# Attention beside an MLP on one core: the last six steps, the order of the last four units, and the projection as a chain

## The chip, the cores and the metric

The kernel runs on one core of one Trainium2 chip. The metric is the device time in microseconds of one execution; the median of the runs shown below is the time before. The profile is one profiled execution; its rows give microseconds from the start of the span, which runs from the first to the last instruction.

## The reference, cut to what matters

Both branches start from `x` (2048 tokens, 576 features) and are mixed by a gate per token:

```python
g = _sigmoid((x * gate_w).sum(-1, keepdims=True))
qkv = (x @ wqkv).reshape(B, S, 3, 32, 18)              # q, k, v of 32 heads of 18
p = _softmax(einsum("bhqd,bhkd->bhqk", q, k) * 18**-0.5)
a = einsum("bhqk,bhkd->bhqd", p, v) (heads joined) @ wo
y = _layernorm(x)
b = _gelu(y @ w1 + b1) @ w2 + b2                       # 576 -> 4608 -> 576
return g * a + (1 - g) * b
```

All is float32. The kernel splits operands into a rounded part and a rest and adds three products of them for one float32 product, so that a matmul line of the code stands for three passes.

## The kernel before, in words

**Prologue.** The first part computes q, k and v for all tokens and stores them to scratch in DRAM (`qk_scr`, `v_scr`), normalizes `x` and stores that too (`y_scr`). It ends where the attention loop begins.

**The loop.** Heads are taken in 16 pairs. A unit `u` is one pair and one half of the queries (1024 of them), so there are 32 units: `unit(u)` gives pair `u // 2` and half `u % 2`. Each unit has 16 steps `kc`, one for each 128 keys; `step` counts through all 512. A step makes scores with `s2` (L236, tile `pss`) and the exponential on ScalarE (L238, into `p` or `ring`). Every second step also runs `pv` (L253, 16 matmuls), which multiplies the probabilities of two steps with v. What follows calls the stretch from one `pv` to the next a double step: 256 of them make the loop. The row maxima that the exponential needs come one unit ahead, from `next_round` (matmul L195, maximum on VectorE L197); when a unit's are complete they are turned by one matmul (L212) and written into the query tile by four small DMAs (`qa<-mr`), which the first scores of the next unit wait for. The score tile `pss` exists once, so scores, exponential and next scores alternate.

**Tiles of the loop.** Queries lie in three tiles `QA`, keys in two tiles `KA` (pair modulo 2), values in two tiles `VT`. `o_store` copies a finished unit's sums out (`oe`), sends them to `ot_scr`, gathers the sums of the exponentials (`dn<-oe`), takes reciprocals on VectorE (L276), writes them out (`dn_scr<-dn`) and spreads them over the rows of all 18 features (`wide`, `ot_scr<-dn_scr`). The two steps behind it wait 24 and 16 slots of `run_due`, in the last two units 4 and 4.

**The MLP beside it.** `mlp()` is a generator; `fill` takes one piece of it three times in each double step. For each of 4 blocks of 512 tokens and 9 groups of the hidden width there are two `h_pair` (L441, 54 matmuls each, weights `w`, tokens `big`) and four `out_pair` (L521, 24 times two matmuls each). A double step holds a whole `h_pair` (54 matmuls, three pieces), or half of one (28, then 26, five pieces over two double steps), or one `out_pair` (48 matmuls). The rule for the first cut is time: `behind` is the MLP time that should have been spent by this step if it were to end at step `FIN`, and an `h_pair` that isn't late is cut into five:

```python
behind[0] = base + (TOTAL - base) * step / FIN        # in fill; FIN = 500
late = spent[0] < behind[0]
if last and piece[0] == 0 and not late:
    ends = {4, 9, 14, 18, 23}
```

Between two blocks the next block's tokens are read in 12 DMAs (`big<-y_scr`).

**The projection.** `out_proj` multiplies the attention output with `wo`. For each block `b` of 512 tokens it loads the sums (`load_o`) and the reciprocals (`load_den`), multiplies and splits them in five chunks (`normed`: VectorE L941, ScalarE L945, VectorE L952), and then runs 8 groups of 14 matmuls (L999), each evicted by VectorE with gate and MLP output (L1003). That makes 32 groups, 448 matmuls. Before, it is appended to the stream when the MLP is done, its loads are tied to four fixed steps, and it takes 3 groups (`PEND`) up to the end of the loop. Block 0 waits until the first 31 units are stored, blocks 2 and 3 until all are. The chunks 0 to 3 are the rows 0 to 511 of `ot_scr`; chunk 4 is the rows 512 to 575, which with the pair size of 36 rows belong to pairs 14 and 15.

**Order of the work.** Nothing is scheduled by a planner: the instructions of each engine run in the order in which the code issues them. `run_due` is called after each piece of the loop (a slot), and it runs what `defer` and `bg` have queued. All DMAs but the output's go through SyncE's queue in that order, so one that waits holds those behind it.

Of the kernel before, what the change touches and what calls it, by code (L numbers as in the profile page):

```python
# [22 lines left out]
NT = S // P  # L23
NB = 4
# [14 lines left out]
PEND = 3  # L39
WAIT = 0.25  # L40
NSL = 1
# [4 lines left out]
PLAN = [[(), (0,), (1,), (2,), (3,), (4,), (5, 6), ()], [(), (), (0,), (1,), (2,), (3,), (4,), (5, 6)],  # L46
        [(0,), (1,), (2,), (3,), (4,), (5,), (6,), ()]]
NORM = 8
# [5 lines left out]
NSTEP = 512  # L54
FIN = NSTEP - 12


@with_exitstack
def gated_mix_kernel(ctx: ExitStack, tc: tile.TileContext, x, wqkv, wo, w1, b1, w2, b2, gate_w, out):
# [36 lines left out]
    KA = [att.tile([P, S], F32R, name=f"ka{i}") for i in range(2)]  # L96
# [33 lines left out]

    def run_due(ns=SLOT):

        slot[0] += 1
        now[0] += ns
        due = [f for t, f in timed if t <= now[0]]
# [21 lines left out]
    NU = 2 * NPAIR  # L157
    NR = 32

    def unit(u):  # L160
        return u // 2, u % 2
# [10 lines left out]
    def load_k(pair, c0=0, c1=S):  # L172
        ka = KA[pair % 2]
# [11 lines left out]
    def s1_round(u, r):  # L185
# [5 lines left out]
        qa, ka = QA[u % 3], KA[u // 2 % 2]  # L191
# [36 lines left out]
    def s2(u, kc, qb):  # L228
        qa, ka = QA[u % 3], KA[u // 2 % 2]
# [12 lines left out]
    def pv(n):  # L242
# [4 lines left out]
        v = VT[u // 2 % 2]  # L247
# [12 lines left out]
    def o_store(u, ps):  # L260
# [14 lines left out]
        def spread():  # L275
            nc.vector.reciprocal(dn, dn)  # L276
            nc.sync.dma_start(dn_scr[u], dn)
            defer(16 if u < NU - 2 else 4, wide)
# [5 lines left out]
        defer(24 if u < NU - 2 else 4, spread)  # L284
# [15 lines left out]
    def mlp():  # L300
# [35 lines left out]
        def more_raws():  # L336

            more = cw.tile([P, 2, D], F32, name="wlast")
            for c in (2, 3):
                R2.append(more[:, c - 2, :])  # L340
# [76 lines left out]
        def h_pair(q, last, inner=False):  # L417
# [17 lines left out]
            if last and piece[0] == 0 and not late:  # L435
# [161 lines left out]
    opening = []  # L597
    stream = [mlp()]
# [33 lines left out]
    with ExitStack() as a:  # L632
# [160 lines left out]
        for i in range(2):  # L793

            nc.gpsimd.memset(VT[i], 0.0)
            for j in range(2):
                nc.gpsimd.memset(VT[i][:, :, 19 * j + 18:19 * j + 19], 1.0)
                nc.gpsimd.memset(KA[i][64 * j + 32:64 * j + 64, :].bitcast(F32), 1.0)
# [75 lines left out]
    hooks = []  # L874
# [3 lines left out]
    def out_proj():  # L878

        wbig = big_tile().rearrange("p a b -> p (a b)").rearrange("p (c n) -> p c n", n=D)  # L880
        wlast = cw.tile([P, 2, D], F32R, name="wlast")
        raw = x_tile().rearrange("p (c n) -> p c n", n=640)[:, :, :D]

        def w_part(hl, c):
            return wbig[:, 5 * hl + c, :] if 5 * hl + c < 8 else wlast[:, c - 3, :]

        def split(c):
            src = raw[:, c % 4, :]
            nc.gpsimd.tensor_scalar(w_part(0, c), src, 1.0, 1.0, op0=ALU.mult, op1=ALU.mult)
            nc.gpsimd.tensor_tensor(w_part(1, c), src, w_part(0, c).bitcast(F32), op=ALU.subtract)  # L890

        def load_last():
            for h in range(2):
                nc.sync.dma_start(raw[64 * h:64 * h + 64, 0, :], wo[512:576, :])

        nc.sync.dma_start(raw, wo[0:512, :].rearrange("(c p) n -> p c n", p=P))
        bg.append((lambda: 0, lambda: split(0), SLOT))
        bg.append((lambda: 0, load_last, SLOT))
        for c in range(1, 5):
            bg.append((lambda: 0, lambda c=c: split(c), SLOT))  # L900
        OT, BT, done = {}, {}, {}

        def load_o(b):

            o = x_tile().rearrange("p (c n) -> p c n", c=5)
            cols = slice(b * TB, (b + 1) * TB)
            nc.sync.dma_start(o[:, 0:4, :], ot_scr[0, 0:512, cols].rearrange("(c p) n -> p c n", p=P))
            for h in range(2):
                nc.sync.dma_start(o[64 * h:64 * h + 64, 4, :], ot_scr[0, 512:576, cols])
            OT[b] = [o]  # L910
            done[b] = 0

        def load_den(b):

# [184 lines left out]
```

## Time and profile before

| | us |
|---|---|
| median of 3 runs (lowest, highest) | 2386.05 (2380.69, 2387.30) |
| the profiled execution | 2386.83 |
| its span | 2385.1 |
| TensorE busy | 2317.6 (97%) |
| VectorE, ScalarE, GpSimd busy | 1648.9, 1365.1, 964.5 |
| the chain that ended last: share of TensorE | 89% |

The profiled execution is 0.78 us above the median, and 1.73 us of it lie outside its span. In a row of the timeline stand the start, the length, the engine, the line of the code, the operation with output and inputs, the number of instructions merged into the row, and in brackets the idle time before it with what ended it. Rows that give a stretch of time list the stretch, its length, the busy time of TensorE's matmuls, of its weight loads, of VectorE, ScalarE and GpSimd with the number of instructions, the granted TensorE clock (1.00 is full speed), the share of the DMA engines and GB/s.

### The profile page before, as it was taken

What the parts mean: (1) busy time and instruction counts of PE and PEld (TensorE: products, weight loads), DVE (VectorE), ACT (ScalarE), POOL (GpSimd) and SP (SyncE); (2) the same over time, 40 slices, a digit from 0 to 9 for tenths busy, and PEclk for the clock granted to TensorE, in tenths of its full rate; (3) what the DMA queues carried; (4) which work ended last, traced back from release to release, by engine and by line L of the source; (5) the groups of instructions that cost most, each with busy time, mean ns of one, the idle gap of its engine ahead of it and who ended that gap; (6) DMA issues with size and microseconds to landing.
All of it is one profiled execution on the core that took longest, in us unless ns stands there. A gap on an engine that the chain in (4) does not pass through costs nothing.

```text
span 2385.1 us, 50611 instructions
## 1 busy us (share of the span) xinstructions
PE 2317.6 (97%) x20585; PEld 1618.2 (68%) x20585; DVE 1648.9 (69%) x2890; ACT 1365.1 (57%) x1604; POOL 964.5 (40%) x964
## 2 busy tenths in 40 slices
PE   8998899999999999999999999999999999999978
PEld 6876566666666666666666666666666676666638
DVE  5675577777777777777777777777766777777424
ACT  4222476666666665666666666666655666666551
POOL 3000466665555333344444443333433344444400
PEclk9999899999999999999999999999999999999989
DMA  7747936544355425242354423232645342331146
GB/s 232 244 145 202 266 130 183 165 144 140 127 157 161 145 93 155 95 132 94 114 153 142 127 97 112 87 112 93 160 117 185 100 124 96 101 126 68 61 149 205
DMA packets 164638, 330.40 MB, mean 139 GB/s; under 512 B 57742, under 2 KB 84402, under 8 KB 153570
## 3 DMA queue, kind: packets, MB, share of 16 engines
q1 hardware_dynamic: 161414, 321.71, 43.5%
q10 hardware_dynamic: 2992, 5.46, 0.6%
q8 instruction: 162, 2.65, 0.5%
q14 instruction: 70, 0.57, 0.1%
HBM read 234.31 MB, written 96.73 MB: 139 GB/s over the span
## 4 chain that ended last, share of the span: by engine, by line
PE 89%; DVE 3%; DMA 3%; ACT 2%; issue 1%; POOL 1%; SPq 0%; ACTq 0%; DVEq 0%; POOLq 0%
PE ps L521 20%; PE ps L253 19%; PE ps L441 17%; PE pss L236 12%; PE ps L195 11%; PE ps L758 4%; PE ps L776 2%; PE ps L999 2%; DVE m L197 1%; ACT p L238 1%; PE ps L682 1%; DMA vt<-v_scr 1%; DMA qa<-mr 0%; DMA big<-y_scr 0%; DVE p L742 0%
## 5 line engine op out<-in xcount | busy, mean ns | idle before, releaser
L197 DVE TENSOR_REDUCE m<-ps 128x1 f32<-128x512 f32 x2048 | 1298.7, 684 | 448.4 <-PE ps L195 447.3
L238 ACT ACTIVATE p<-pss 128x1024 f32<-128x1024 f32 x684 | 701.0, 1025 | 471.3 <-PE pss L236 457.8
L441 PE MATMUL ps<-big,w 64*128 64x512 f32 x3888 | 518.7, 393 | 3.2 <-DMA big<-y_scr 3.1
L154 POOL TENSOR_SCALAR zz<-zz 128x512 f32<-128x512 f32 x288 | 178.3, 619 | 829.7 <-ACT zz L494 727.3
L521 PE MATMUL ps<-w,hh 64*128 64x288 f32 x4352 | 497.1, 299 | 12.0 <-ACT z L462 0.3
L236 PE MATMUL pss<-qa,ka 56*128 56x512 f32 x2048 | 481.5, 437 | 25.3 <-ACT p L238 13.8
L238 ACT ACTIVATE ring<-pss 128x1024 f32<-128x1024 f32 x340 | 348.5, 1025 | 241.2 <-PE pss L236 236.0
L195 PE MATMUL ps<-ka,qa 54*128 54x512 f32 x2048 | 457.9, 410 | 6.2 <-DVE m L197 2.6
L521 PEld LDWEIGHTS ps<-w,hh 64*128 64x128 f32 x4352 | 398.5, 185 | 68.0 <-issue 44.6
L441 PEld LDWEIGHTS ps<-big,w 64*128 64x128 f32 x3888 | 394.0, 185 | 68.1 <-DMA big<-y_scr 3.9
L236 PEld LDWEIGHTS pss<-qa,ka 56*128 56x128 f32 x2048 | 198.0, 185 | 281.4 <-ACT p L238 127.3
L154 POOL TENSOR_TENSOR zz<-zz,z 128x512 f32<-128x512 f32 x288 | 371.6, 1290 | 24.1
L253 PE MATMUL ps<-p,vt 128*32 128x512 f32 x2736 | 351.2, 608 | 0.4 <-DMA vt<-v_scr 0.4
L521 PE MATMUL ps<-w,hl 64*128 64x288 f32 x2176 | 349.0, 292 | 0.0
L195 PEld LDWEIGHTS ps<-ka,qa 54*128 54x128 f32 x2048 | 239.7, 185 | 36.1 <-DVE m L197 11.9
L521 PEld LDWEIGHTS ps<-w,hl 64*128 64x128 f32 x2176 | 233.8, 185 | 0.3
L154 POOL TENSOR_TENSOR w<-x,w 128x1152 fp32r<-128x1152 f32 (+1 forms) x36 | 73.1, 2044 | 325.9 <-ACT w L357 312.6
L253 PE MATMUL ps<-ring,vt 128*32 128x512 f32 x1360 | 181.4, 606 | 0.0
L154 POOL TENSOR_TENSOR hl<-zz,hh 128x512 fp32r<-128x512 f32 x136 | 176.6, 1299 | 11.4
L253 PEld LDWEIGHTS ps<-p,vt 128*32 128x32 f32 x2736 | 72.1, 110 | 151.7 <-issue 150.3
L530 DVE SCALAR_TENSOR_TENSOR x<-ps,x 128x288 f32<-128x288 f32 x256 | 105.1, 452 | 33.2 <-PE ps L521 19.6
L758 PE MATMUL ps<-big,wqk 128*128 128x512 f32 x504 | 126.8, 405 | 0.8 <-DVE wqk L676 0.5
(95 smaller groups left out, 1363.3 us busy)
## 6 DMA issues: line engine op xcount, KB each, us to landing
w<-w_scr SPq DMA_DIRECT2D x54, 1152.0 KB
w<-w_scr SPq DMA_DIRECT2D x108, 576.0 KB
w_scr<-w SPq DMA_DIRECT2D x18, 1152.0 KB
w_scr<-w SPq DMA_DIRECT2D x36, 576.0 KB
big<-y_scr SPq DMA_DIRECT2D x42, 384.0 KB
x<-in_B_w_dram SPq DMA_DIRECT2D x54, 288.0 KB
qa<-qk_scr SPq DMA_DIRECT2D x192, 72.0 KB
ka<-qk_scr SPq DMA_DIRECT2D x90, 144.0 KB
```

What stands on the lines that cost most here:

```text
L154: fn(*args, **kw)
L195: nc.tensor.matmul(ps, qa[r0:r0 + 54, t * P:(t + 1) * P], ka[r0:r0 + 54, kb * TB:(kb + 1) * TB], start=True, stop=True)
L197: nc.vector.tensor_reduce(M4[u][:, h, t, kb:kb + 1], ps, axis=AX.X, op=ALU.max)
L236: nc.tensor.matmul(ps[:, h, :], ka[r0:r0 + 56, kc * P:(kc + 1) * P], qa[r0:r0 + 56, qb * TB:(qb + 1) * TB], start=True, stop=True)
L238: nc.scalar.activation(RING[n % 3][:, qb], ps, AF.Exp, scale=SCALE)
L253: nc.tensor.matmul(OB[u][r:r + 32, :], v[:, k, 19 * h:19 * h + 32], RING[c % 3][:, qb, h, :], start=(k == 0), stop=(k == NT - 1))
L441: nc.tensor.matmul(ps[h], wt[w_][r, c, :], Y[s_][r, c, :], start=(k == 0), stop=(k == 26))
L521: nc.tensor.matmul(ps[nn][:, :ND], h_[r, tok], w_[p_][r, cs[nn]], start=(k == 0), stop=(k == 6 * G - 1))
L530: nc.vector.scalar_tensor_tensor(dst, ps[nn][:, :ND], 0.5, b2b[:, cs[nn]] if g == 0 else dst, op0=ALU.mult, op1=ALU.add)
L758: nc.tensor.matmul(ps, w_[:, c, ms], big[:, s_, :], start=(k == 0), stop=(k == len(prods) - 1))
L776: nc.tensor.matmul(ps[:, :ND], big[:, s_, tok], w_[:, c, cs], start=(k == 0), stop=False)
L999: nc.tensor.matmul(ps[:, :ND], OT[b][2][:, s_, tok], w_part(w_, c)[:, cs], start=(k == 0), stop=(k == 13))
```

## The change

The MLP is spread up to step 506 instead of 500 (`FIN`), and an `h_pair` is also cut into five where the MLP is more than 3200 ns ahead (`AHEAD`). The units 29 and 30 change places, so that both pairs 14 and 15 have their first halves done by unit 29; for that there is a third key tile, and pair 15's keys are loaded a unit earlier. The reciprocals of unit 29 take the short delays too. The projection's steps are a list `chain`, of which `run_due` runs at most one per slot once its condition holds: the weights `wo` are loaded from step 472, block 0 as soon as 30 units are stored, blocks 2 and 3 first without chunk 4, and chunk 4 when all is stored. `fill` gives it seven matmuls per interval. Its groups use the banks of `ps_s1` and `ps_w` in turn, and its output tiles are two instead of three. The diff, cut to its core:

```diff
-PEND = 3
-WAIT = 0.25
-NSL = 1
-PLAN = [[(), (0,), (1,), (2,), (3,), (4,), (5, 6), ()], ...]
-NORM = 8
+PLAN = [(), (), (0,), (1,), (2,), (3,), (4, 5), (6,)]
+PROJ = 7
+EARLY = NSTEP - 40
-FIN = NSTEP - 12
+FIN = NSTEP - 6
+AHEAD = 3200.0
...
-    KA = [att.tile([P, S], F32R, name=f"ka{i}") for i in range(2)]
+    KA = [att.tile([P, S], F32R, name=f"ka{i}") for i in range(3)]
...
     def run_due(ns=SLOT):
         slot[0] += 1
         now[0] += ns
+        if chain and chain[0][0]():
+            chain.pop(0)[1]()
...
+    UNITS = [divmod(u, 2) for u in range(NU)]
+    UNITS[NU - 3:NU - 1] = UNITS[NU - 2], UNITS[NU - 3]
     def unit(u):
-        return u // 2, u % 2
+        return UNITS[u]
...
-            defer(16 if u < NU - 2 else 4, wide)
+            defer(16 if u < NU - 3 else 4, wide)
...
-        defer(24 if u < NU - 2 else 4, spread)
+        defer(24 if u < NU - 3 else 4, spread)
...
-            if last and piece[0] == 0 and not late:
+            if (last or spent[0] > behind[0] + AHEAD) and piece[0] == 0 and not late:
                 ends = {4, 9, 14, 18, 23}
...
+        for i in range(3):
+            for j in range(2):
                 nc.gpsimd.memset(KA[i][64 * j + 32:64 * j + 64, :].bitcast(F32), 1.0)
...
+        def load_o(b, first=True, last=True):
+            if first:
+                o = x_tile().rearrange("p (c n) -> p c n", c=5)
+                ka, qa = {0: (KA[1], QA[2]), 1: (KA[1], QA[2]), 2: (KA[2], QA[0]), 3: (KA[1], QA[2])}[b]
...
+            o, den, ka = OT[b][:3]
+            rows((o[:, 0:4, :], o[:, 4, :]), 0, b, first, last)
+            rows((ka.bitcast(F32).rearrange("p (c n) -> p c n", c=4), den[4]), 1, b, first, last)
...
+        def late():
+            load_o(2, first=False)
+            load_o(3, first=False)
+
+        then(lambda: at[0] >= EARLY, load_wo)
+        then(lambda: len(stored) >= NU - 2, lambda: load_o(0))
+        then(lambda: hidden[0] == NB - 1, split_wo)
         for c in range(7):
-            defer(NSL * c, lambda c=c: normed(0, c))
+            then(after(2), lambda c=c: normed(0, c))
+        then(lambda: opened[0] and len(stored) >= NU - 1, lambda: 0)
+        then(after(16), lambda: load_o(2, last=False))
+        then(after(12), lambda: 0)
+        for c in range(6):
+            then(after(0), lambda c=c: normed(2, c, range(4)))
+        then(lambda: done[1] == 5, lambda: load_o(3, last=False))
+        then(lambda: len(stored) == NU, late)
+        then(after(3), lambda: 0)
+        for c in range(4, 7):
+            then(after(0), lambda c=c: normed(2, c, (4,)))
+        for c in range(6):
+            then(after(0), lambda c=c: normed(3, c, range(4)))
+        for c in range(4, 7):
+            then(after(0), lambda c=c: normed(3, c, (4,)))
...
-        cbig = ctx.enter_context(tc.tile_pool(name="c_big", bufs=1))
-        io = ctx.enter_context(tc.tile_pool(name="c_io", bufs=3))
+        cbig = ctx.enter_context(tc.tile_pool(name="c_big", bufs=2))
+        io = ctx.enter_context(tc.tile_pool(name="c_io", bufs=2))
+        while 0 not in done or done[0] < 5:
+            run_due()
+        load_b(0)
+        load_o(1)
+        opened[0] = True
...
-                    ps = psum(ps_s1)
+                    ps = psum((ps_s1, ps_w)[banks % 2])
...
-            if not stream and step > NSTEP - NORM:
+            if not stream:
                 stream.append(proj)
-                over[0] = step
+                over[0] = 3 * (step // 2) + share
...
-            filler(PEND * 14 * 122.5 * (step + 1 - over[0] - WAIT) / (NSTEP - over[0] - WAIT))
+            filler(PROJ * 122.5 * (3 * (step // 2) + share - over[0]))
...
+                elif u == NU - 5:
+                    load_k(NPAIR - 1)
+                elif u == NU - 4:
+                    load_v(NPAIR - 1)
```

In the changed kernel the lines stand a little lower: scores are L240, `pv` L257, the MLP's matmuls L445 and L525, the projection's L1022. Three places show how instructions move.

TensorE, the end of the loop, before: the last piece of the MLP (L521) and the double steps behind it, scores (L236), `pv` (L253) and the projection (L999).

```order
L521 MATMUL ps<-w_29054,w_29013 128x288 x12
L236 MATMUL pss<-qa_104,ka_107 128x512 x2
L253 MATMUL ps<-p,vt_109 32x512 x8
L236 MATMUL pss<-qa_104,ka_107 128x512 x8
L253 MATMUL ps<-ring_2347,vt_109 32x512 x4
L253 MATMUL ps<-p,vt_109 32x512 x4
L236 MATMUL pss<-qa_104,ka_107 128x512 x8
L253 MATMUL ps<-p,vt_109 32x512 x4
L253 MATMUL ps<-ring_2347,vt_109 32x512 x4
L236 MATMUL pss<-qa_104,ka_107 128x512 x6
L999 MATMUL ps<-big 128x288 x5
L236 MATMUL pss<-qa_104,ka_107 128x512 x2
```

The same place after:

```order
L525 MATMUL ps<-w_29189,w_29160 128x288 x12
L240 MATMUL pss<-qa_104,ka_106 128x512 x2
L257 MATMUL ps<-p,vt_110 32x512 x8
L240 MATMUL pss<-qa_104,ka_106 128x512 x4
L1022 MATMUL ps<-big 128x288 x7
L240 MATMUL pss<-qa_104,ka_106 128x512 x2
L1022 MATMUL ps<-big 128x288 x3
L1022 MATMUL ps<-wlast,big 128x288
L1022 MATMUL ps<-big 128x288 x2
L1022 MATMUL ps<-wlast,big 128x288
L240 MATMUL pss<-qa_104,ka_106 128x512 x2
L257 MATMUL ps<-ring_2350,vt_110 32x512 x4
```

Six `pv` follow the MLP's last piece before, the first two and a half of them with nothing between the scores; after, three follow, and seven matmuls of the projection stand in every interval but the first.

SyncE's queue at the change from the third to the fourth block of the MLP, before (`big<-y_scr`: the block's tokens; `qa<-mr`: the row maxima of the next unit):

```order
L113 DMA w_21951<-w_scr 128x2304
L282 DMA ot_scr<-dn_scr 36x1x1024
L113 DMA big<-y_scr 64x3x512 x12
L113 DMA qa_105<-mr 1x8x128 x4
L267 DMA dn<-oe 128x1x16
```

and after:

```order
L111 DMA w_22002<-w_scr 128x2304
L286 DMA ot_scr<-dn_scr 36x1x1024
L111 DMA qa_105<-mr 1x8x128 x4
L111 DMA big<-y_scr 64x3x512 x12
L271 DMA dn<-oe 128x1x16
```

The four small DMAs now stand ahead of the twelve large ones, because the MLP reaches this change a double step later while the units stay where they are.

SyncE's queue at the end, before: from the last unit's sums on (`dn<-oe`; `ot_scr<-dn_scr` is the spreading of the reciprocals; `x` and `ka`, `qa` are a block's sums and reciprocals).

```order
L267 DMA dn<-oe 128x1x16
L273 DMA ot_scr<-oe 18x512 x4
L907 DMA x<-ot_scr 128x4x512
L909 DMA x<-ot_scr 64x512 x2
L277 DMA dn_scr<-dn 128x16
L282 DMA ot_scr<-dn_scr 36x1x1024
L920 DMA ka_107<-ot_scr 128x4x512
L923 DMA qa_104<-ot_scr 64x512 x2
```

and after:

```order
L929 DMA x<-ot_scr 128x4x512
L929 DMA ka_108<-ot_scr 128x4x512
L271 DMA dn<-oe 128x1x16
L277 DMA ot_scr<-oe 18x512 x4
L281 DMA dn_scr<-dn 128x16
L947 DMA bt<-b_scr 128x4x576
L286 DMA ot_scr<-dn_scr 36x1x1024
L929 DMA x<-ot_scr 128x4x512
L929 DMA ka_107<-ot_scr 128x4x512
L932 DMA x<-ot_scr 64x512 x2
L932 DMA qa_103<-ot_scr 64x512 x2
```

Block 2's chunks 0 to 3 now stand ahead of the last unit's sums, block 3's behind the spreading of its reciprocals, and only chunk 4 of both behind these.

More of the change, by code (lines that the diff above doesn't have):

```diff
@@ L336, in more_raws @@
         def more_raws():
-            more = cw.tile([P, 2, D], F32, name="wlast")
+            W["raw"] = cw.tile([P, 3, D], F32, name="wraw")
             for c in (2, 3):
-                R2.append(more[:, c - 2, :])
+                R2.append(W["raw"][:, c - 2, :])
                 load_w2(c)
@@ new lines, in out_proj, with then, after, due @@
+        OT, BT, done, tmp = {}, {}, {}, {}
+        def then(cond, fn):
+            chain.append((cond, fn))
+        def after(n):
+            base = []
+            def due():
+                if not base:
+                    base.append(slot[0])
+                return slot[0] >= base[0] + n
+            return due
+        def w_part(hl, c):
+            return W["big"][:, 5 * hl + c, :] if 5 * hl + c < 8 else W["last"][:, c - 3, :]
+        def load_wo():
+            nc.sync.dma_start(W["raw"], wo[0:384, :].rearrange("(c p) n -> p c n", p=P))
@@ L1069, in gated_mix_kernel @@
     pv(NSTEP - 2)
-    hooks[0]()
-    while stream or later or timed:
+    while stream or later or timed or chain:
         filler(spent[0] + 1000.0)
```

137 lines of the change are left out of this document (55 added, 82 removed).

## The prediction

> **What bounds the kernel now.** I read the page's busy shares first, then busy time by stage, then TensorE's timeline from one `pv` to the next, and last the timelines of SyncE and VectorE behind the loop.
>
> ```profile
> span 2385.1 us, 50611 instructions
> ...
> PE 2317.6 (97%) x20585; PEld 1618.2 (68%) x20585; DVE 1648.9 (69%) x2890; ACT 1365.1 (57%) x1604; POOL 964.5 (40%) x964
> ...
> 269.00:2269.00 2000.00, 1977.20 (x18714) 1354.35 (x18714) 1448.68 (x2503) 1252.03 (x1433) 927.18 (x937) 1.00 0.41 127
> 2269.00:2321.00 52.00, 38.80 (x202) 14.71 (x200) 9.55 (x17) 28.48 (x32) 0.74 (x1) 0.80 0.46 159
> 2321.00:2386.00 65.00, 56.87 (x412) 55.58 (x406) 32.22 (x59) 9.78 (x16) 0.00 (x0) 0.95 0.57 191
> ```
>
> TensorE carries the time, but not alike everywhere. From 269 to 2269 us it is busy for 99% at full clock. From 2269 to 2321 us, where the MLP is over and the loop goes on, it is busy for three quarters at a clock of 0.80, with 202 matmuls in 52 us against 9.4 per us before. Behind the loop (65 us) it is busy for 87%. So the waste lies in the last 117 us; what can be moved into it from the full part is a gain.
>
> **The price of a double step.** The rows are the starts of `pv` at well-behaved places.
>
> ```profile
> 2183.81 1.07 PE L253 MATMUL ps<-ring,vt 128*32 128x512 f32 x8
> ...
> 2198.55 1.92 PE L253 MATMUL ps<-p,vt 128*32 128x512 f32 x16
> ...
> 2206.13 1.06 PE L253 MATMUL ps<-ring,vt 128*32 128x512 f32 x8
> ...
> 2213.72 1.06 PE L253 MATMUL ps<-p,vt 128*32 128x512 f32 x8
> ...
> 2223.94 1.92 PE L253 MATMUL ps<-p,vt 128*32 128x512 f32 x16
> ...
> 2246.66 1.92 PE L253 MATMUL ps<-p,vt 128*32 128x512 f32 x16
> ...
> 2268.98 1.92 PE L253 MATMUL ps<-p,vt 128*32 128x512 f32 x16
> ...
> 1798.39 1.06 PE L253 MATMUL ps<-ring,vt 128*32 128x512 f32 x8
> ...
> 1816.85 1.92 PE L253 MATMUL ps<-p,vt 128*32 128x512 f32 x16
> ```
>
> An `h_pair` over two double steps (28 and 26 matmuls) takes 2198.55 - 2183.81 = 14.74 us; a whole one in one double step (54) 2223.94 - 2213.72 = 10.22; an `out_pair` (48) 2213.72 - 2206.13 = 7.59, and without row maxima (2268.98 - 2246.66) / 3 = 7.44. An irregular pair of double steps (34, then 20 + 48) takes 18.46.
>
> **Part 1, the MLP to step 506.** In the order of both programs I counted the double steps up to the last MLP piece: 249 before, 252 after. After, there are two fewer with 54, three more pairs of 28 and 26, one more with 48 without maxima, and the irregular pair is gone: -20.44 + 44.22 + 7.44 - 18.46 = +12.76 us. Three more double steps thus cost 12.8 us in place of about 22, since pieces leave the crowded ones. The `pv` behind the MLP's last piece moves from 2268.98 to 2281.74, and three double steps are left instead of six.
>
> **Part 2, a stall that goes with the shift.** At the third block change the trace has this (TensorE, then SyncE there, then SyncE at the second change):
>
> ```profile
> 1729.03 1.06 PE L253 MATMUL ps<-p,vt 128*32 128x512 f32 x8
> ...
> 1740.40 0.84 PE L236 MATMUL pss<-qa,ka 56*128 56x512 f32 x2 [3.96 <-DMA qa<-mr]
> ...
> 1750.18 1.07 PE L253 MATMUL ps<-ring,vt 128*32 128x512 f32 x8
> ...
> 1715.51 10.23 SPq L113 DMA_DIRECT2D big<-y_scr  x12
> 1727.00 6.79 SPq L113 DMA_DIRECT2D qa<-mr  x4
> ...
> 1214.92 0.63 SPq L113 DMA_DIRECT2D qa<-mr  x1
> 1215.65 10.52 SPq L113 DMA_DIRECT2D big<-y_scr  x12
> ```
>
> The scores wait for four small DMAs queued behind twelve large ones. Those two double steps (48, then 28) take 21.15 us; their kinds take 7.59 + 7.37 = 14.96. At the second change the small ones stood in front, as they do at the third after the change. So -6.2 us, between 0 (the stall comes at another place) and -6.2; I take all of it, since in the new order no `qa<-mr` stands behind the large ones. The `pv` behind the MLP is then due at 2275.5.
>
> **Part 3, the last three double steps.**
>
> ```profile
> 2276.17 0.80 PE L236 MATMUL pss<-qa,ka 56*128 56x512 f32 x2 [1.18 <-ACT p L238]
> ...
> 2296.60 2.60 PE L253 MATMUL ps<-p,vt 128*32 128x512 f32 x16
> ...
> 2319.24 2.30 PE L253 MATMUL ps<-p,vt 128*32 128x512 f32 x16
> ...
> 2276.00:2280.00 4.00, 3.83 (x18) 0.88 (x18) 0.00 (x0) 1.14 (x2) 0.00 (x0) 0.50 0.70 263
> ```
>
> With nothing between the scores TensorE waits 1.18 us per exponential, its clock falls to 0.50, and the first three of these take (2296.60 - 2268.98) = 27.6 us, the next three, with 12 or 13 projection matmuls each, 22.6. After, three are left with 14, 21 and 21 matmuls (56 instead of 42 up to the last `pv`). Bounds: 22.0 if the clock holds (7.44 twice and a last one without two of its scores, some 7.1), 27.6 if it falls as before. I take 22.0: the filling is nearer to the second three, and denser. The last `pv` starts at 2297.5 and ends 1.9 later, at 2299.4.
>
> The Trainium skill (TensorE: Matmul & The Clock Gate, "What's actually happening") says that the clock drops to half only after an idle window of about 3.4 us. Here it fell with gaps of 1.18 us, so the trace disagrees; by the rule alone these steps would cost 22.0 without doubt, and the upper end would go.
>
> **Part 4, behind the loop.**
>
> ```profile
> 2323.43 1.48 PE L999 MATMUL ps<-big 128*128 128x288 f32 x10
> ...
> 2340.17 1.49 PE L999 MATMUL ps<-big 128*128 128x288 f32 x10
> ...
> 2345.19 2.27 PE L999 MATMUL ps<-big 128*128 128x288 f32 x10 [3.00 <-DVE res L1003]
> ...
> 2381.00 0.30 PE L999 MATMUL ps<-wlast,big 128*128 128x288 f32 x1
> ```
>
> A group of 14 takes (2340.17 - 2323.43) / 9 = 1.86 us. After, 28 groups are left (29 before): 52.1 us. The wait of 3.00 us, for block 2's reciprocals, goes; what is late next is chunk 4 of block 2. Its chain before:
>
> ```profile
> 2322.31 0.62 SPq L267 DMA_DIRECT2D dn<-oe  x1
> ...
> 2327.39 0.60 SPq L277 DMA_DIRECT2D dn_scr<-dn  x1
> 2334.22 0.66 SPq L282 DMA_DIRECT2D ot_scr<-dn_scr  x1
> ...
> 2340.16 1.11 SPq L923 DMA_DIRECT2D qa<-ot_scr  x2
> ...
> 2344.02 0.69 DVE L941 TENSOR_TENSOR x<-x,ka 128x512 f32<-128x512 f32 x1 [6.85 <-DMA ka<-ot_scr]
> ...
> 2352.00:2360.00 8.00, 7.58 (x56) 7.23 (x55) 3.53 (x7) 1.26 (x2) 0.00 (x0) 1.00 1.05 372
> ```
>
> From the loop's end (2321.1) to the issue of chunk 4's reciprocals are 19 us; with at most 3.9 us to land (2340.16 to 2344.02; taken as 3) and 2.5 for the product (0.69, the row above), two copies (0.57 each, a row below) and the rest (as long as the product), chunk 4 is ready 24.6 us behind the loop. TensorE needs it after 12 groups and 12 matmuls: 22.3 + 1.6 = 23.9. So the wait is 0.7 us if the chain runs as before. But after, 2 MB for block 2 stand ahead of `dn<-oe` and 2 MB for block 3 ahead of chunk 4; at the 372 GB/s of the last row 2 MB are 5.6 us. The chain before also had a block's loads in it, so I take 3 of 0 to 8 us.
>
> From the last matmul (2381.3) to the span's end are 3.8 us, as before.
>
> **Small parts.**
>
> ```profile
> 9.26 1.80 POOL L798 MEMSET ka<- 32x2048 f32 x1
> 22.78 3.31 POOL L676 TENSOR_TENSOR wqk<-p,wqk 128x1440 fp32r<-128x1440 f32 x1 [11.72 <-ACT wqk L675]
> ...
> 2284.65 1.02 ACT L238 ACTIVATE ring<-pss 128x1024 f32<-128x1024 f32 x1 [0.67 <-PE pss L236]
> ...
> 2287.54 1.14 ACT L945 ACTIVATE big<-x 128x512 fp32r<-128x512 f32 x2
> ```
>
> The third key tile adds two memsets of 1.80 us on GpSimd, which then waits 11.72 us: nothing; without that cover 3.6. Block 0's six copies on ScalarE (0.57 each) move into full double steps. They fit into the 0.67 us between exponentials; between 0 and 3.4 us, taken as 1. Unit 29's reciprocals are due half a double step behind its sums while the maxima go on behind them on VectorE: `dn<-oe` to reciprocal took 5.1 us above (2322.31 to 2327.39), half a double step is 3.8, so 1.3 us of VectorE, between 0 and 1.3 for TensorE, taken as 1. Block 0's loads (2.4 MB, 6.3 us at that rate) are issued about a double step behind unit 29 and stand ahead of the last `qa<-mr`, which follows some four double steps later; nothing. The weights' splits on GpSimd and their loads only move to earlier idle time: nothing. Two output tiles instead of three: a tile is needed again after two groups' rest, 3.7 us; nothing to 2, in the 3 above.
>
> **The sum.** 2299.4 + 52.1 + 3 + 3.8 + 1 + 1 = 2360.3, which is 24.8 us under the span of 2385.1. The profiled execution (2386.83) is 0.8 us above the median of 2386.05; from the median I come to 2361 us.
>
> **Rivals.**
>
> The last unit's chain is late (A). If `dn<-oe` waits for both blocks' loads and chunk 4 for 2 MB more, the wait is 8 to 12 us instead of 3, and the clock then falls for a few us: 2366 to 2372. For it: the four small DMAs at 1727.00 landed at 1740.40, behind large ones. Against it: between MLP and loop's end lie 22 us in which the loads can land. The Trainium skill (DMA: Bandwidth & Descriptors, "Queues, rings and completion order") says that each DMA engine takes a queue's descriptors in order, which those rows bear out. By that rule alone `dn<-oe` lands behind block 2's 2 MB, 5.6 us later than taken, and the time would be 2367.
>
> The shift only moves stalls (B): part 2 returns at another block change, where block loads and unit loads meet (after the change a unit's six query loads stand between the twelve at the first), or the steps at low clock stay. +6.2 or +5.6: 2367.
>
> The shift brings nothing (C): double steps with 28 or 26 are bound by scores and exponentials at 7.37, so pieces moved into steps of their own cost a whole double step. Then part 1 gives +22, with the rest as above: 2370. Against it: the double steps with 54 take 10.22, well over 7.37, and two of them go.
>
> Slower (D): VectorE's queue has block 1's first product ahead of the last unit's sums and of the fourth group's eviction. Block 1's sums wait for the MLP's last output to be stored. If they land late, TensorE runs on until five banks are full (group 8, 7.5 us behind the loop) and then each us costs one. It decides from a landing some 35 us behind the loop's end; 45 us would give 2396. Against it: the MLP ends 22 us before the loop, and the loads are 4.7 MB, 12.6 us at 372 GB/s.
>
> **How the numbers follow.** Forecast 0.62, A 0.2, B 0.08, C 0.06, D 0.04. A measurement here can tell about 0.3%, 7.2 us: faster means under 2378.9. The first four are all faster, unless two of them come together (0.04 for no change). The forecast's own range is 2354 to 2367: all costs taken as above zero (3 + 1 + 1) gone and a little in the pieces, or the wait at 8. For 8 in 10 it reaches into A, B and C, and on the lower side by the 0.2% that the runs before scatter: 2351 to 2374.
>
> **What would show it.** The double steps with 54 fall by two; no wait for `qa<-mr` of some 4 us near 1740; MLP's end near 2275 and the last `pv` near 2297; clock at 0.9 or more in the last three double steps; a wait of 0 to 8 us before block 2's chunk 4 some 24 us behind the loop. The prediction is wrong if the `pv` behind the MLP isn't near 2275, or if TensorE waits over 10 us behind the loop.

## The result and the profile after

| | us |
|---|---|
| median of 4 runs after (lowest, highest) | 2366.68 (2365.69, 2367.84) |
| before, beside it | 2385.70 |
| ratio, with its 95% interval | 0.9926 (0.9913 to 0.9938) |
| the profiled execution after, its span | 2367.84, 2365.9 |

The change makes the kernel 19 us faster. 2361 was forecast; the time lies 5.7 us above it, inside the range of 2351 to 2374. The page of the changed kernel: span and busy times.

```profile
span 2365.9 us, 50603 instructions
PE 2310.1 (98%) x20585; PEld 1616.1 (68%) x20585; DVE 1650.9 (70%) x2890; ACT 1365.2 (58%) x1604; POOL 969.4 (41%) x966
```

Busy time by stage (columns as before): loop with the MLP, loop behind the MLP, behind the loop.

```profile
271.00:2278.00 2007.00, 1986.84 (x18787) 1354.75 (x18783) 1457.45 (x2513) 1266.94 (x1452) 928.73 (x936) 1.00 0.41 127
2278.00:2301.00 23.00, 21.40 (x143) 11.32 (x135) 3.32 (x7) 13.22 (x14) 0.75 (x1) 1.00 0.95 324
2301.00:2366.00 65.00, 54.63 (x392) 53.99 (x392) 31.88 (x58) 9.67 (x16) 0.00 (x0) 0.95 0.46 162
```

The stage behind the MLP has shrunk from 52 to 23 us and runs at a clock of 1.00 instead of 0.80, busy for 93% instead of 75%. The stage behind the loop is as long as it was, though it has a group of matmuls less: TensorE is busy there for 54.6 us of 65.

TensorE's timeline, starts of `pv` (now L257): the loop's first, two around the third block change, the one behind the MLP's last piece, the loop's last; then SyncE at that block change.

```profile
270.68 3.64 PE L257 MATMUL ps<-p,vt 128*32 128x512 f32 x16 [0.65 <-DMA vt<-v_scr]
...
1728.24 1.07 PE L257 MATMUL ps<-p,vt 128*32 128x512 f32 x8
...
1743.47 1.07 PE L257 MATMUL ps<-ring,vt 128*32 128x512 f32 x8
...
2277.61 1.92 PE L257 MATMUL ps<-p,vt 128*32 128x512 f32 x16
...
2299.06 1.93 PE L257 MATMUL ps<-p,vt 128*32 128x512 f32 x16
...
1720.28 2.71 SPq L111 DMA_DIRECT2D qa<-mr  x4
1723.09 10.53 SPq L111 DMA_DIRECT2D big<-y_scr  x12
```

The small loads stand in front of the large ones, and the two double steps there take 1743.47 - 1728.24 = 15.23 us where they took 21.15. The last three double steps take 2299.06 - 2277.61 = 21.45 us.

Behind the loop, TensorE's waits, then the last unit's way on SyncE (with its reciprocal on VectorE), then the row of VectorE that waits for chunk 4 of block 2.

```profile
2311.59 0.37 PE L1022 MATMUL ps<-big 128*128 128x288 f32 x1 [1.39 <-DVE big L969]
...
2331.76 0.58 PE L1022 MATMUL ps<-big 128*128 128x288 f32 x1 [5.06 <-DVE big L969]
...
2332.38 2.60 PE L1022 MATMUL ps<-big 128*128 128x288 f32 x10
...
2301.76 0.62 SPq L271 DMA_DIRECT2D dn<-oe  x1
...
2306.55 0.25 DVE L280 RECIPROCAL dn<-dn 128x16 f32<-128x16 f32 x1
...
2311.22 0.65 SPq L286 DMA_DIRECT2D ot_scr<-dn_scr  x1
2311.98 0.63 SPq L929 DMA_DIRECT2D x<-ot_scr  x1
2312.66 0.86 SPq L929 DMA_DIRECT2D ka<-ot_scr  x1
...
2319.63 2.58 SPq L932 DMA_DIRECT2D qa<-ot_scr  x2
...
2329.35 0.69 DVE L957 TENSOR_TENSOR x<-x,qa 128x512 f32<-128x512 f32 x1 [6.54 <-DMA qa<-ot_scr]
```

TensorE waits 1.39 us for block 1's last chunk and 5.06 us for chunk 4 of block 2, and then its clock is down (ten matmuls in 2.60 us instead of 1.49), which costs some 2 us more by the third group behind it. The two rows at 2311.98 and 2312.66 are the 2 MB for block 3, ahead of chunk 4's reciprocals in the queue.

### The profile page after: what moved, and what is told of

It is laid out like the page before. It is cut to its first block, busy times and chain, and to the rows that moved or that the text cites. A ratio compares the mean times of both kernels' runs of the same rounds, so it can differ in the third digit from the quotient of the medians.

```text
span 2365.9 us, 50603 instructions
## 1 busy us (share of the span) xinstructions
PE 2310.1 (98%) x20585; PEld 1616.1 (68%) x20585; DVE 1650.9 (70%) x2890; ACT 1365.2 (58%) x1604; POOL 969.4 (41%) x966
## 4 chain that ended last, share of the span: by engine, by line
PE 89%; DVE 4%; DMA 2%; ACT 2%; issue 1%; POOL 1%; SPq 0%; ACTq 0%; DVEq 0%; POOLq 0%
PE ps L525 20%; PE ps L257 19%; PE ps L445 17%; PE pss L240 13%; PE ps L199 11%; PE ps L763 4%; PE ps L781 2%; PE ps L1022 1%; DVE m L201 1%; ACT p L242 1%; DMA vt<-v_scr 1%; PE ps L687 1%; DMA w_scr<-w 0%; DVE p L747 0%; POOL w L156 0%
## 5 line engine op out<-in xcount | busy, mean ns | idle before, releaser
L445 PE MATMUL ps<-big,w 64*128 64x512 f32 x3888 | 520.7, 393 | 3.3 <-DMA big<-y_scr 3.2
L525 PE MATMUL ps<-w,hh 64*128 64x288 f32 x4352 | 495.4, 299 | 11.7
L240 PE MATMUL pss<-qa,ka 56*128 56x512 f32 x2048 | 479.1, 436 | 11.0 <-ACT p L242 7.0
L525 PEld LDWEIGHTS ps<-w,hh 64*128 64x128 f32 x4352 | 396.3, 186 | 67.8 <-issue 44.6
L445 PEld LDWEIGHTS ps<-big,w 64*128 64x128 f32 x3888 | 393.4, 186 | 68.8 <-DMA big<-y_scr 4.1
L240 PEld LDWEIGHTS pss<-qa,ka 56*128 56x128 f32 x2048 | 196.4, 184 | 265.2 <-ACT p L242 124.4
L257 PE MATMUL ps<-p,vt 128*32 128x512 f32 x2736 | 346.2, 601 | 0.6 <-DMA vt<-v_scr 0.6
L525 PE MATMUL ps<-w,hl 64*128 64x288 f32 x2176 | 346.4, 292 | 0.0
L525 PEld LDWEIGHTS ps<-w,hl 64*128 64x128 f32 x2176 | 230.9, 185 | 0.5
L156 POOL TENSOR_TENSOR hl<-zz,hh 128x512 fp32r<-128x512 f32 x136 | 176.8, 1300 | 11.3
L257 PE MATMUL ps<-ring,vt 128*32 128x512 f32 x1360 | 179.1, 598 | 0.0
L257 PEld LDWEIGHTS ps<-p,vt 128*32 128x32 f32 x2736 | 71.6, 109 | 149.9 <-issue 148.7
```

The source lines that it names most:

```text
L156: fn(*args, **kw)
L240: nc.tensor.matmul(ps[:, h, :], ka[r0:r0 + 56, kc * P:(kc + 1) * P], qa[r0:r0 + 56, qb * TB:(qb + 1) * TB], start=True, stop=True)
L257: nc.tensor.matmul(OB[u][r:r + 32, :], v[:, k, 19 * h:19 * h + 32], RING[c % 3][:, qb, h, :], start=(k == 0), stop=(k == NT - 1))
L445: nc.tensor.matmul(ps[h], wt[w_][r, c, :], Y[s_][r, c, :], start=(k == 0), stop=(k == 26))
L525: nc.tensor.matmul(ps[nn][:, :ND], h_[r, tok], w_[p_][r, cs[nn]], start=(k == 0), stop=(k == 6 * G - 1))
```

## Experiments

Unless it says otherwise, an edit is made to the changed kernel, and "behind the loop" counts from the start of the last `pv`. The runs were made in five batches, each with the kernel before beside them. Its median lay between 2383.50 and 2385.70 us, so times from different batches compare to about 2 us; the ratios are to the kernel before of the same batch.

### What chunk 4 waits for

**Chunk 4 first.**

```diff
-        then(lambda: done[1] == 5, lambda: load_o(3, last=False))
-        then(lambda: len(stored) == NU, late)
+        then(lambda: len(stored) == NU, lambda: load_o(2, first=False))
+        then(lambda: done[1] == 5, lambda: load_o(3, last=False))
+        then(lambda: 3 in OT, lambda: load_o(3, first=False))
```

> The changed kernel, but chunk 4 of block 2 is loaded ahead of block 3's chunks 0 to 3 instead of behind them. Queue theory (the wait of 5.06 us before block 2's chunk 4, and the slow clock of 2.4 us behind it, come from 2 MB and outputs ahead of 256 KB in the queue): chunk 4 is ready some 25 us behind the loop instead of 30.8, the wait is 0 to 1 us, the clock holds, and the time is 2359 to 2361 us. Chain theory (gathering, reciprocals and spreading take that long by themselves): the wait stays at 4 to 5 us and the time within 1 us of 2366.7.

Measured: 2360.78 us, ratio 0.9904 (0.9891 to 0.9918). The same places in its timelines (`pv`, SyncE, VectorE, TensorE):

```profile
2299.94 1.92 PE L257 MATMUL ps<-p,vt 128*32 128x512 f32 x16
...
2312.10 0.65 SPq L286 DMA_DIRECT2D ot_scr<-dn_scr  x1
...
2320.50 1.08 SPq L932 DMA_DIRECT2D qa<-ot_scr  x2
2321.67 0.54 SPq L929 DMA_DIRECT2D x<-ot_scr  x1
...
2325.46 0.69 DVE L957 TENSOR_TENSOR x<-x,qa 128x512 f32<-128x512 f32 x1 [0.78 <-DMA qa<-ot_scr]
...
2328.56 0.37 PE L1023 MATMUL ps<-big 128*128 128x288 f32 x1 [0.98 <-DVE big L969]
```

The reciprocals are issued 20.56 us behind the loop, as in the changed kernel (2319.63 - 2299.06 = 20.57), but are used 25.5 us behind it instead of 30.3. The wait is 0.98 us and the clock stays up. So the order costs 5 to 6 us: 5.9 by the medians, and 5.1 from the last `pv` to the span's end in the two profiles (66.8 and 61.8 us).

**By bytes or by semaphores?** In the changed kernel SyncE's waits for the loads of chunk 4 name the output stores (9.8 us in four) beside the spread (`ot_scr<-dn_scr`, 2.0 us), as if its loads shared semaphores with the stores in ScalarE's queue. So the stores were moved:

```diff
-                nc.scalar.dma_start(out[tt * P:(tt + 1) * P, :], res)
+                nc.gpsimd.dma_start(out[tt * P:(tt + 1) * P, :], res)
```

> The changed kernel with one word changed: the output stores are issued from GpSimd instead of ScalarE, so that SyncE's loads no longer wait for semaphores that these stores hold. Semaphore theory: SyncE's four loads for block 2's chunk 4 leave at once behind the 2 MB for block 3 (2313.5 instead of 2315.4 to 2324), the chunk is ready at about 2324, TensorE needs it at 2326.3; the wait of 5.06 us and the 2.4 us of low clock behind it go: 2359 us (2358 to 2361). Rival (the chunk waits for bytes, 2 MB for block 3 ahead of it, whenever it is issued): within 1.5 us of 2366.7. If a store from GpSimd itself takes longer, output tiles come free later and VectorE waits: above 2367.

Measured: 2367.13 us, ratio 0.9922 (0.9910 to 0.9934).

```profile
2297.18 1.92 PE L257 MATMUL ps<-p,vt 128*32 128x512 f32 x16
...
2317.68 1.11 SPq L932 DMA_DIRECT2D qa<-ot_scr  x2
...
2327.88 0.69 DVE L957 TENSOR_TENSOR x<-x,qa 128x512 f32<-128x512 f32 x1 [7.20 <-DMA qa<-ot_scr]
...
2330.29 0.58 PE L1022 MATMUL ps<-big 128*128 128x288 f32 x1 [5.49 <-DVE big L969]
```

The issue stands 20.5 us behind the loop again and the use 30.7. No load of SyncE behind the loop waits for the stores any more, and the time is the same, so the semaphore theory falls: the loads leave when the last unit's spread, which they read, has landed (SyncE's wait right ahead of them is the one for `ot_scr<-dn_scr`, 2.8 us), and then take 10.2 us to their use behind block 3's 2 MB.

**Normalisation earlier**, alone and with chunk 4 first:

```diff
-PLAN = [(), (), (0,), (1,), (2,), (3,), (4, 5), (6,)]
+PLAN = [(), (0,), (1,), (2,), (3,), (4,), (5, 6), ()]
```

> The changed kernel with block 1's normalisation spread one group earlier (PLAN moved by one group). Theory: the 1.39 us that TensorE waits for block 1's last chunk is a wait on VectorE's order of work and goes: 2365.3 us. Rival (VectorE is full there, 7.9 of 8 us busy, so the wait only comes at another group): 2366.7 within 0.5.

> Both edits: chunk 4 of block 2 loaded ahead of block 3's 2 MB, and block 1's normalisation one group earlier. If the gains add: 2360.8 - 1.4 = 2359.4 us; if VectorE is full there: 2360.8.

Measured: 2366.31 us, ratio 0.9914 (0.9902 to 0.9927), and 2360.34 us, ratio 0.9889 (0.9877 to 0.9902). The first wait goes in both, and the one for chunk 4 grows by as much or more; here of the one, then of the other:

```profile
2334.28 0.58 PE L1022 MATMUL ps<-big 128*128 128x288 f32 x1 [6.87 <-DVE big L969]
```

```profile
2326.25 0.37 PE L1023 MATMUL ps<-big 128*128 128x288 f32 x1 [2.55 <-DVE big L969]
```

Both gains fail for one reason: chunk 4 comes as long behind the loop as without the edit (32.9 us against 32.7, and 28.6 against 28.6), so what TensorE gains ahead of it comes back as waiting. The traces show this; the times alone could not, since the first kernel's runs lie between 2362.78 and 2371.09 us. The second version is nominally the fastest of this study, and not to be told from the one with chunk 4 first alone.

**The next block's MLP rows later.** 1.15 MB (`bt`) stand ahead of the spread, so in addition:

```diff
-            if b + 1 < NB:
-                load_b(b + 1)
+            if b == 0:
+                load_b(1)
             for t in range(4):
+                if t == 2 and 0 < b < NB - 1:
+                    load_b(b + 1)
```

> Chunk 4 first and normalisation earlier, and in addition the MLP rows of the next block (1.15 MB, bt) loaded in the middle of a block instead of at its start, so that they don't stand ahead of the last unit's spread on SyncE, where they also waited 3.5 us for an eviction. Byte theory: the spread is issued about 1.5 us earlier and lands about 3 us sooner, the wait of 2.55 us before chunk 4 goes: 2360.3 - 2.5 = 2357.8 us. Rival (the spread's round trip through DRAM sets the time, not what stands ahead of it): 2360.3 within 0.7; if bt itself then comes late for block 2's first evictions: above 2361.

Measured: 2363.47 us, ratio 0.9916 (0.9901 to 0.9931).

```profile
2306.94 0.65 SPq L286 DMA_DIRECT2D ot_scr<-dn_scr  x1
...
2312.41 1.08 SPq L932 DMA_DIRECT2D qa<-ot_scr  x2
...
2323.89 0.52 DVE L1029 SCALAR_TENSOR_TENSOR res<-ps,gate,bt 128x288 f32<-128x288 f32 x1 [4.89 <-DMA out_dram<-res]
...
2327.42 0.37 PE L1025 MATMUL ps<-big 128*128 128x288 f32 x1 [3.66 <-DVE big L969]
...
2334.30 0.52 DVE L1029 SCALAR_TENSOR_TENSOR res<-ps,gate,bt 128x288 f32<-128x288 f32 x1 [7.03 <-DMA bt<-b_scr]
```

The loads of chunk 4's reciprocals now leave 14.7 us behind the loop (the last `pv` starts at 2297.74), but their product stands in VectorE's queue behind an eviction that waits 4.89 us for an output store. TensorE waits 3.66 us for the chunk, where it waited 2.55, and its clock falls behind that (ten matmuls in 2.20 us). `bt` does come late, as the last case of the expectation has it, and VectorE waits 7.03 us for it; but TensorE has no wait from 2327.42 on, so in this profile that wait is not what makes the time longer. The number of the last case came, its mechanism did not.

**The first filled step.** As the one before, with `over[0]` one less:

> As the one before, and the projection in the loop starts with a full share: 14 more of its matmuls stand between the scores behind the MLP, 70 instead of 56, so that no gap of 1.18 us is left there. In the loop they lie beside exponentials that take the step's time anyway; behind it 1.86 us go. Theory: 1.9 us less than the run before, 2356; and if the 1.18 us gap is what lets the clock fall in some executions, their scatter (6 to 8 us between the fastest and the slowest) becomes smaller. Rival (the steps grow by what is put into them, since they are full): the same time within 0.7.

Measured: 2363.60 us, ratio 0.9917 (0.9903 to 0.9932), the same as without it. ScalarE and TensorE in the third step:

```profile
2293.69 0.63 ACT L960 ACTIVATE big<-x 128x512 fp32r<-128x512 f32 x1 [1.75 <-DVE x L957]
...
2295.28 0.50 PE L240 MATMUL pss<-qa,ka 56*128 56x512 f32 x2 [0.94 <-ACT p L242]
```

The three steps grow from 21.42 to 23.21 us. The trace has 63 matmuls of the projection in them against 56, so the edit moves 7 and not the 14 that were expected. Seven are 0.93 us; a wait of 0.94 us for an exponential, which stands behind a copy of the projection on ScalarE, is the rest. Nothing is gained, as the rival said, but only half of the growth is what was put in. A gap of 1.18 us is left even so, and the scatter is unchanged (2.1 us in four runs each).

### The stall at the third block change

**The small loads in front, in the kernel before.** A first try loaded the next block's rows in one go behind the pair:

```diff
-                if change and (k + 1 in ends or k == 26):
+                if change and k == 26:
+                    while ROWS:
+                        ROWS.pop(0)()
```

> The kernel before with one edit: at a block change the next block's rows are loaded in one go behind the last matmul of the pair, and the waiting row of maxima is sent ahead of them; at the third change SyncE then issues the four small qa<-mr in front of the large loads. On TensorE one transposition moves by one place. Stall theory: those two double steps take 15.2 us instead of 21.2, and nothing takes the time back: 2384.9 - 5.6 = 2379.3 us (2378.5 to 2380.5). Rival (the stall is given back later, at the MLP's end or behind the loop): 2384.9 within 1.5.

Measured: 2414.34 us, ratio 1.0122 (1.0102 to 1.0142). The double step in which the scores had waited takes 7.67 instead of 12.15 us, but the large loads themselves now come late at all three changes. TensorE's waits for them in the whole program (us in total, times, longest; before 3.1 us in two):

```profile
PE ps L441 <- DMA big<-y_scr: 29.5, 9, 6.0
```

Six of the nine lie at the changes and last 24.8 us together. So this edit bought one wait with six others and says nothing on the theory. The second try keeps the large loads' times and only puts the four small ones behind eight of twelve:

```diff
                 if change and (k + 1 in ends or k == 26):
+                    while k == 26 and ROWS:
+                        ROWS.pop(0)()
```

> The kernel before with one edit, at the third block change alone: the four small qa<-mr are issued behind eight of the twelve large loads instead of behind all twelve; the large ones keep their time. On TensorE one transposition moves by one place. Stall theory: the small loads are issued some 4 us earlier and have 1.5 MB less ahead of them, so the two double steps take 15.3 to 17 us instead of 21.2, and the time is 4 to 6 us under that of before (2384 in most runs, so 2378 to 2380). Rival (the stall is given back at the MLP's end or behind the loop): the same time as before within 1.5 us.

Measured: 2379.65 us against 2385.63 of the kernel before, ratio 0.9978 (0.9969 to 0.9987).

```profile
1728.67 1.07 PE L253 MATMUL ps<-p,vt 128*32 128x512 f32 x8
...
1743.72 1.06 PE L253 MATMUL ps<-ring,vt 128*32 128x512 f32 x8
...
1714.88 5.31 SPq L113 DMA_DIRECT2D big<-y_scr  x8
1720.76 4.47 SPq L113 DMA_DIRECT2D qa<-mr  x4
1726.42 6.78 SPq L113 DMA_DIRECT2D big<-y_scr  x4
```

15.05 us instead of 21.15, and 6.0 us in the time: the stall is worth what it lasts, and nothing gives it back.

### The spread of the MLP

**MLP as before**, with all the rest changed, and **spread without running ahead**:

```diff
-FIN = NSTEP - 6
-AHEAD = 3200.0
+FIN = NSTEP - 12
+AHEAD = 1e9
```

> The changed kernel with the MLP placed as before (end at step 500, no cut when ahead), all else changed. The projection then fills six double steps (119 matmuls) instead of three (56). My theory: the stall at the third block change is back (6.2 us), the six double steps take 7.3 us each at full clock, and the loop ends at about 2314 with 43.7 us of matmuls left, but block 2's chunk 4 is ready only 25 to 31 us behind the loop while TensorE needs it after 15.6: a wait of 9 to 15 us, 2372 to 2380 us in all. Rival (behind the loop nothing but matmuls counts): no wait, about 2362 to 2364 us.

```diff
-AHEAD = 3200.0
+AHEAD = 1e9
```

> The changed kernel with the MLP still spread to step 506, but no first halves running ahead (AHEAD so large that it never applies). At the third block change the twelve large loads then stand in front of the four small ones again. Stall theory: the two double steps there take 20.8 us instead of 15.2, 5.6 more; two more double steps with 54 matmuls, and two fewer with MLP pieces behind them, cost about 5.5 us in the loop and give it back as 42 more projection matmuls (5.6 us) ahead of the loop's end; so 2372 to 2373 us. Rival (the plan of pieces takes up the stall, since pieces are dealt by shares of the work done): within 1 us of 2366.7.

Measured: 2379.55 us, ratio 0.9975 (0.9965 to 0.9985), and 2380.40 us, ratio 0.9976 (0.9967 to 0.9984). From the starts of `pv`, the spans (the profiled execution of the first is 4.3 us under its median), and the order of the programs:

| us | before | after | MLP as before | no run-ahead |
|---|---|---|---|---|
| first `pv` to the one behind the MLP | 1999.85 | 2006.93 | 1999.67 | 2006.05 |
| double steps left, and their time | 6: 50.26 | 3: 21.45 | 6: 46.63 | 5: 40.97 |
| projection matmuls in them | 42 | 56 | 119 | 98 |
| last `pv` to the span's end | 65.9 | 66.8 | 60.4 | 65.8 |
| the two steps at the third change | 21.15 | 15.23 | 20.80 | 20.70 |

Both have the stall back, since without running ahead the large loads again come in front of the small ones. The spread alone brings nothing over the MLP as before; running ahead is what turns it into time, by the stall and by two double steps with 54 matmuls fewer. The first lies inside the time that was expected, with a wait of 8.27 us for chunk 4 where 9 to 15 were expected. My expectation for the second missed by 8 us, because of what its profile shows at the end (TensorE's two waits, then the stretch around the first):

```profile
2305.30 0.80 PE L240 MATMUL pss<-qa,ka 56*128 56x512 f32 x2 [2.49 <-ACT ring L242]
...
2346.04 0.58 PE L1022 MATMUL ps<-big 128*128 128x288 f32 x1 [10.55 <-DVE big L969]
```

```profile
2302.00:2308.00 6.00, 3.51 (x21) 1.46 (x23) 4.69 (x8) 3.78 (x6) 0.00 (x0) 0.68 0.00 0
```

The exponentials are held up by copies of the projection queued on ScalarE, the clock falls, and chunk 4 costs 10.55 us: with 42 more matmuls done in the loop (5.6 us) TensorE needs it sooner, while it comes only 1.6 us earlier (31.1 us behind the loop, 32.7 in the changed kernel). Most of the matmuls moved into the loop come back as this wait. In both kernels block 3's 2 MB and `bt` stand ahead of small transfers of the last unit. Without running ahead, 11.6 us pass from the 8 KB write of the reciprocals to the spread (4.4 in the changed kernel); with the MLP as before, 8.6 us from `dn<-oe` to the reciprocals (4.8).

### The filling and the order of the units

**No projection in the loop.**

```diff
-PROJ = 7
+PROJ = 0.01
```

> The changed kernel with one projection matmul in the last three double steps instead of 56. If gaps of 1.2 us let the clock fall, as the trace of before shows, these three take 26 to 28 us instead of 21.5 and the loop ends 6 us later; with 447 matmuls left (59.4 us) chunk 4 is no longer waited for: 2369 to 2372 us. If the clock falls only after idle windows of 3.4 us (the Trainium skill, TensorE: Matmul & The Clock Gate), the three take 22 us and the time is 2363 to 2366 us, no slower than the changed kernel.

Measured: 2376.64 us, ratio 0.9968 (0.9957 to 0.9980). The stretches behind the MLP:

```profile
2276.00:2284.00 8.00, 4.79 (x29) 1.60 (x25) 0.05 (x1) 4.18 (x5) 0.75 (x1) 0.78 0.79 279
2284.00:2292.00 8.00, 4.85 (x22) 1.00 (x14) 0.00 (x0) 3.47 (x4) 0.00 (x0) 0.71 1.01 318
2292.00:2300.00 8.00, 5.59 (x22) 1.35 (x22) 0.00 (x0) 3.12 (x4) 0.00 (x0) 0.66 0.89 326
```

With bare scores the clock falls, as before, and the three steps take 25.15 us instead of 21.45. Beside these 3.7 us, the last `pv` takes 1.6 us longer at the low clock, the four groups that were in the loop cost 7.4 behind it, and the waits there are 1.7 us shorter (2.40 us for chunk 4 and 2.40 for block 1, against 5.06 and 1.39). That makes 11.0 us; from the first `pv` to the span's end the two profiles differ by 11.4 us, and the medians by 10.0. The expectation had counted the groups, but no waiting behind the loop; 4.8 us of it are left, since chunk 4 comes 40.5 us behind the loop here, hence the miss. The fall of the clock itself is as its first case said.

**Units in their old order.** The swap of `UNITS` is taken out, and block 0 is loaded when 31 units are stored instead of 30.

> The changed kernel with the units in their old order; block 0 is then loaded when 31 units are stored instead of 30. Cover theory: the MLP covers block 0's loads and splits either way (unit 30 is stored some four double steps before the MLP ends), so the time is that of the changed kernel within 2 us. Rival (the order of the units makes block 0 come in time): TensorE waits for block 0 in the last three double steps, the clock falls, and the time is 2372 to 2380 us.

Measured: 2371.72 us, ratio 0.9948 (0.9935 to 0.9960). VectorE, then TensorE:

```profile
2254.90 0.69 DVE L956 TENSOR_TENSOR x<-x,ka 128x512 f32<-128x512 f32 x1 [11.87 <-DMA ka<-ot_scr]
2255.51 0.81 DVE L533 SCALAR_TENSOR_TENSOR x<-ps,x 128x288 f32<-128x288 f32 x2
...
2256.01 1.21 PE L524 MATMUL ps<-w,hh 64*128 64x288 f32 x4 [3.46 <-DVE x L533]
```

My theory that other work covers it fell. Block 0's first product is in VectorE's queue before its data have landed, the evictions of an `out_pair` stand behind it, and that double step takes 13.22 us instead of 7.34. The rival did not come as stated either: the last three double steps wait for nothing of block 0 and take 21.4 us at a clock of 1.00; the loss lies inside the MLP. The swap moves the load to where it has time to land.

## Why the prediction was right, and where its size was off

- **Part 1 and 2, the shift and the stall: right.** From the first `pv` to the one behind the MLP the time grew by 2006.93 - 1999.85 = 7.08 us; predicted were 12.76 - 6.2 = 6.56. In the traces the double steps with 54 matmuls fall from 36 to 34. The stall's share is shown by the run with four loads between (6.0 us). Rival B (stalls only move) is out.
- **Rival C (a shifted piece costs a whole step): out.** Three more double steps with the MLP cost 7.08 + 5.9 = 13.0 us, not 22. But the run without running ahead shows how near it lay: there two double steps with 54 stay, and nothing is won.
- **Part 3, three steps: right.** 21.45 us against 22.0, at a clock of 1.00. Without the filling they take 25.15, inside the bound of 27.6.
- **Part 4, the wait: the mis-sized term.** 3 us were taken for chunk 4, of 0 to 8. The wait measured 5.06. The step that failed is the landing: I took 3 us, since before it took at most 3.9, and of the 5.6 us for 2 MB ahead I added only 2.3 (a wait of 3 us in place of 0.7). From the loop's end (2300.9) to the issue it is 18.7 us, as predicted (19); from issue to use 9.72 us, which falls to 4.96 when block 3's 2 MB stand behind. The Trainium skill (DMA: Bandwidth & Descriptors, "Queues, rings and completion order") says that each DMA engine takes a queue's descriptors in order, and those two numbers agree. With the low clock behind it and the wait for block 1's last chunk, which I had not foreseen, 1.39 + 5.06 + 2 = 8.4 us were lost. Rival A had half of the mechanism: the 2 MB ahead of chunk 4, and the low clock. Its other half, a late `dn<-oe`, did not come: block 2's 2 MB were issued by 2290.42, 11.3 us ahead of it, and the reciprocal ran 4.8 us after it (2301.76 to 2306.55), against 5.1 before. So it is luck that the time lies beside A's lower end of 2366 and beside the 2367 that was worked out for a late `dn<-oe`; A's wait of 8 to 12 us did not come.
- **Small parts: 2 us that weren't there.** No wait for ScalarE's copies or unit 29's reciprocals shows on TensorE in the changed kernel's last double steps (7.3 us each). The order of the units, on the other hand, got no price at all, and without the swap the kernel is some 5 us slower. The alternating banks, the two output tiles, unit 29's short delays and a setting that only the full diff has (`dynamic_dma_scratch_size=1024`) were not taken back one by one; what each is worth stays open.
- **Rival D (VectorE's queue behind block 1): not seen.** VectorE waits for no load of block 1 in the changed kernel; the 1.39 us for its last chunk are the order of VectorE's own work, since they go when that is spread one group earlier.
- **The sum.** Span predicted 2360.3, measured 2365.9: +5.4 for the waits, -2 for the small parts, +1.6 since the last `pv` starts at 2299.06 and not at 2297.5, of which 1.55 stand already at the first `pv` (270.68 against 269.13); the rest, 0.6, is spread over the end. The median of 2366.68 lies just inside the forecast's own range of 2354 to 2367: direction and mechanism came, but the gain was 19 us where 25 were forecast.

## What to carry to other kernels

Where the end hangs on one chain of round trips through DRAM, look at what stands ahead of each of its transfers, in bytes; putting one load of 2 MB behind it was worth as much as a third of this whole change. Work moved ahead of such a chain came back mostly as waiting, as long as the chain itself was no shorter. And before spreading work evenly, see whether the pieces' sizes change with it: the spread paid only with the rule that cut the crowded steps.

## What the runs showed of the hardware

- **The same gap did not always cost the clock.** A gap of 1.18 us right behind the MLP is in the profiles of the changed kernel and of every variant. In ten of them the steps behind it are filled; it left the clock at 1.00 in nine, but in the kernel with the earlier normalisation alone the clock fell there:

```profile
2281.00:2286.00 5.00, 4.94 (x24) 3.31 (x26) 0.52 (x1) 2.31 (x3) 0.00 (x0) 0.63 1.05 394
2286.00:2290.00 4.00, 4.00 (x21) 1.02 (x14) 0.00 (x0) 1.02 (x2) 0.00 (x0) 0.61 0.95 301
```

  It cost 2.9 us over two double steps. A gap of 2.55 us behind dense work (chunk 4 first, earlier normalisation) left it at 1.00, while one of 2.40 us at the same chunk (no projection in the loop) did not: the ten matmuls behind it took 2.67 us instead of 1.49. The idle window of about 3.4 us of the Trainium skill (TensorE: Matmul & The Clock Gate, "What's actually happening") agrees with the gap of 2.55 us and not with those of 1.18 and 2.40. The same section says that this window runs freely and isn't aligned with the kernel, so that the same work can change the clock at different points from run to run; the two kernels' different outcomes at the same gap agree with that. No run here shows the window itself, so what decides stays open.
- **A write that is read back.** From the issue of the spread (144 KB) to the issue of the loads that read it are 8.4 us with 1.15 MB ahead of it (8.3 to 9.5 in five profiles), 5.5 us without (one profile).
- **The prologue scatters.** The first `pv` starts at 266.0 to 270.7 us in the profiled executions of kernels with the same prologue; up to 4.7 us of the difference between two profiles arise before the loop begins.
